# Attention and routed experts on one core: the planner models TensorE's clock and places filler products in its idle time

## The chip, the cores and the metric

The kernel runs on one core of a Trainium2 chip. The metric is the device time of the whole kernel in microseconds (us). One core has five engines with queues of their own, each worked off in order: TensorE (PE, with its weight loads shown apart as PEld), VectorE (DVE), ScalarE (ACT), GpSimd (POOL) and SyncE (SP), which here only starts transfers. TensorE runs at one of two clock levels, 2.4 or 1.2 GHz; the profile shows the granted share of the full clock as PEclk (1.00 or 0.50).

## The reference

```python
# q, k, v: 8 batches x 8 heads x 576 positions x 64, float32
def attention(q, k, v):
    q_rot, k_rot = rotate(q), rotate(k)          # rotary embedding, tables of cos and sin
    scores = matmul(q_rot, k_rot.T) / sqrt(64)
    attn = exp(scores - max(scores))             # along the keys
    return matmul(attn / (sum(attn) + 1e-9), v)
x = attention(q, k, v)                           # heads side by side: 8 x 576 x 512
for b in range(8):
    s = x[b] @ w_gate
    top = argpartition(-s, 128)[:128]            # 128 of 576 rows
    y = maximum(x[b, top] @ w1, 0) @ w2          # 512 -> 1024 -> 512
    out[b] = x[b]
    out[b, top] += sigmoid(s[top])[:, None] * y
```

## The kernel before

The work is cut into 32 pairs of heads (8 batches with 4 pairs each). For one pair, `load` brings q, k and v to SBUF, `rotate` applies the rotary embedding on POOL (on DVE for the first pair), and `turn_qk` transposes q and k on TensorE and splits them into a high and a low part (ACT, POOL, DVE), so that three fast products give a float32 result. `attend` then works in nine units of 128 query rows: `units` makes the scores of two units at a time (twelve products, line 569), `softmax` takes the maximum of each row on DVE (line 586) and the exponential on ACT (line 590), and DVE transposes the exponentials in 32x32 blocks (`turn`, line 604). What a block transpose can't do is done by six transfers from SBUF to SBUF, the moves (`move`, line 617, tile `pt`): two first, and two others that wait for these. Then come the value products (`value`, line 646, float32): per pair one group `c=0` and one group `c=1`, each of 36 products on quarters of the array, which the trace shows as 72 MATMUL records, for one float32 product makes two. The result is copied (line 302), transposed back (line 690) together with the gate's products (line 691), and scaled by DVE (lines 701 to 713). There is one `pt` tile of each kind, so the DVE transposes of the next pair wait until the value products have read it. After every fourth pair `route`, `chosen` and `experts_of` select the 128 rows of a batch and send them through the two expert layers (line 911).

No engine's order is written by hand. Every step is an `Op` with the time that its engine is taken by it, the time until its result is there, a key (a due time) and the steps that it needs. `Order.run` plays the whole kernel through with these costs and lets each engine, whenever it is free, take the ready step with the lowest key; the instructions are then issued in the order so found. A step marked urgent (the score units and the softmax) that is soon ready may keep an engine waiting: another step is taken only if it ends at most `over` ns after that moment. The plan decides the order only; on the chip, semaphores decide the times. In PSUM there are eight banks. A step that needs one asks for kind "t" (one bank, from banks 2 to 7) or kind "s" (a pair of banks); the planner gives out the bank that has been free longest, and the program makes TensorE wait until that bank's last reader is through.

The planner's costs that matter here: a group of value products takes `9 * (228 + 55 * c)` ns, so 2.05 us for `c=0` and 2.55 us for `c=1`; a move takes SP 620 ns, and is counted as landed 2000 ns after it is issued; 256 instructions of TensorE are fetched as one block, which is counted as 3900 ns.

```python
o = op({"SP": (620, 2000)},
       lambda: nc.sync.dma_start(flat[32 * to:32 * to + 32, w_to], flat[32 * at_:32 * at_ + 32, w_at]),
```

Of the kernel before, what the change touches and what calls it, by code (L numbers as in the profile page):

```python
# [19 lines left out]
EPS = 1e-9  # L20


KEY = dict(ahead=8500, lag=13000, rem=400, value=4300, rows=3000, load=22300, rotate=115700, half=2500,
           gate=11700, route=58400, count=35500, select=12400, turn=17500, step=7600, kstep=2700, hold=3,
           patience=900, over=300, near=-300, swap=6000, vsplit=9, vstep=0, recip=6000, pool_lo=1, esplit=2, s_pairs=(0, 1, 2, 3), t_banks=(2, 3, 4, 5, 6, 7), t_most=4)

# [12 lines left out]
class Order:  # L39
# [3 lines left out]

    SEM = 45.0
    BLOCK, FETCH = 256, 3900.0
    PER_KB = 3.6


# [22 lines left out]
    def run(self):  # L71
        import heapq

        names = ("PE", "ACT", "DVE", "POOL", "SP")
        free = {e: 0.0 for e in names}
        mode, shared = 0, 0.0
        count, fetched, moving = 0, 0.0, 0.0
        waiting = {e: [] for e in names}
        idle = [0.0] * (2 * self.pairs)
        held = {}  # L80

        def frees(kind):
            if kind == "s":
                return sorted(max(idle[2 * i:2 * i + 2]) for i in KEY["s_pairs"])
            if sum(x >= 1e12 for x in held.values()) >= KEY["t_most"]:
                return []
            return sorted(idle[i] for i in KEY["t_banks"])

        def take(kind):
            if kind == "s":  # L90
                i = min(KEY["s_pairs"], key=lambda i: max(idle[2 * i:2 * i + 2]))
                idle[2 * i] = idle[2 * i + 1] = 1e12
            else:
                i = min(KEY["t_banks"], key=lambda i: idle[i])
                idle[i] = held[i] = 1e12
            return i

        def give(b, t):
            if b.kind == "s":
                idle[2 * b.slot] = idle[2 * b.slot + 1] = t  # L100
            else:
                idle[b.slot] = held[b.slot] = t

        events = [0.0]
        order = []

        def arrive(o):
            for e in o.engines:
                heapq.heappush(waiting[e], (o.key, o.seq, o))
            heapq.heappush(events, o.ready)  # L110

        for o in self.ops:
            if not o.waits:
                arrive(o)
        while events:
            t = heapq.heappop(events)
            while events and events[0] <= t:
                heapq.heappop(events)
            moved = True
            while moved:  # L120
                moved = False
                for e in names:
                    if free[e] > t:
                        continue
                    put, found, soon, first = [], None, None, None
                    while waiting[e]:
                        item = heapq.heappop(waiting[e])
                        o = item[2]
                        if o.done:
                            continue  # L130
                        can, new = o.ready, {}
                        for b in o.banks:
                            if b.slot is None:
                                new[b.kind] = n = new.get(b.kind, 0) + 1
                                at_ = frees(b.kind)
                                can = max(can, at_[n - 1] if n <= len(at_) else 1e12)
                            elif b.last != e:
                                can = max(can, b.free)
                        if can > t:
                            if o.urgent and can < t + KEY["patience"] and (soon is None or can < soon):  # L140
                                soon = can
                        elif soon is None or t + o.engines[e][0] <= soon + KEY["over"]:
                            if e != "PE" or o.mode == mode or o.urgent and first is None:
                                found = o
                                break

                            if first is None:
                                until = o.key + KEY["near"]
                            if first is None or self.TURN.get((mode, o.mode), 0.0) < self.TURN.get((mode, first.mode), 0.0):
                                first = o  # L150
                        put.append(item)
                        if first and o.key > until:
                            break
                    for item in put:
                        heapq.heappush(waiting[e], item)
                    found = found or first
                    if found is None:
                        if soon is not None:
                            heapq.heappush(events, soon)
                        continue  # L160
                    o, moved = found, True
                    if o is first:
                        o.done = True
                    takes, lasts = o.engines[e]
                    begin = t
                    if e == "DVE" and o.mode == 2:
                        begin = max(t, free["POOL"])
                        shared = begin + takes
                    elif e == "POOL":
                        begin = max(t, shared)  # L170
                    if e == "PE":
                        begin += self.TURN.get((mode, o.mode), 0.0) + 70.0 * (t > free[e] + 1)
                        mode = o.mode
                        n, end = o.size, begin
                        while n:
                            if count % self.BLOCK == 0:
                                end = max(end, fetched)
                                fetched = end + self.FETCH
                            step = min(n, self.BLOCK - count % self.BLOCK)
                            end += takes * step / o.size  # L180
                            n, count = n - step, count + step
                        begin += max(0.0, end - begin - takes)
                    if e == "SP":
                        moving = max(moving, begin + takes) + self.PER_KB * o.size
                        begin += max(0.0, moving - begin - takes)
                    for b in o.banks:
                        if b.slot is None:
                            b.slot = take(b.kind)
                    o.done, o.start, o.end = True, t, begin + lasts
                    order.append((t, len(order), o, e))  # L190
                    free[e] = t + takes if e == "SP" else begin + takes
                    heapq.heappush(events, free[e])
                    for b in o.banks:
                        b.left -= 1
                        b.end = max(b.end, o.end)
                        b.last, b.free = e, b.end + self.SEM
                        heapq.heappush(events, b.free)
                        if not b.left:
                            give(b, b.end + self.SEM)
                            heapq.heappush(events, b.end + self.SEM)  # L200
                    for n in o.outs:
                        n.ready = max(n.ready, o.end + self.SEM)
                        n.waits -= 1
                        if not n.waits:
                            arrive(n)
        assert all(o.done for o in self.ops)
        return order
# [24 lines left out]
def attention_moe_kernel(ctx: ExitStack, tc: tile.TileContext, q, k, v, gate, w1, w2, rope, outs, shape, cap):  # L232
# [17 lines left out]
    nc = tc.nc  # L250
# [19 lines left out]
    def sb(name, shape, dtype=F32):  # L270
        return const.tile(shape, dtype, name=name)
# [6 lines left out]
    order = Order(4)  # L278
    op = order.op
# [26 lines left out]
    def bank_of(b):  # L306
        return banks[:, b.slot] if b.kind == "t" else banks[:, 2 * b.slot:2 * b.slot + 2]


    ident = sb("ident", [P, P])  # L310
    make_identity(nc, ident)
    tabs = sb("tabs", [P, 3, NS, D // 2])
# [30 lines left out]
    rows = ring("row", 1, [P, S])  # L343
# [202 lines left out]
    def attend(pi):  # L546
# [64 lines left out]
        def move(c, key, turns):  # L611
# [1 line left out]
            flat = pt[c].tile.rearrange("p w m s j -> p w (m s j)")  # L613

            def part(to, w_to, at_, w_at, needs):
                o = op({"SP": (620, 2000)},
                       lambda: nc.sync.dma_start(flat[32 * to:32 * to + 32, w_to], flat[32 * at_:32 * at_ + 32, w_at]),  # L617
                       key, needs, size=144 + 36 * c)
                pt[c].by(o)
                moved[c].append(o)  # L620
                return o
# [102 lines left out]
        step = PAIR / len(UNITS)  # L724
        lag = KEY["lag"]
# [366 lines left out]
```

## Time and profile before

| | |
|---|---|
| median of 3 runs | 699.35 us (699.29 to 708.92) |
| the profiled execution | 699.43 us, of which 697.7 us from the first to the last instruction |
| mean granted TensorE clock | 0.951 |
| instructions | 19908, of which PE and PEld 7696 each |

The span is what the trace covers; 1.7 us lie around it. Busy times are unions of an engine's records; TensorE's ends are modelled, so its busy time holds some waiting. A group of rows names the engine's line, the tiles written and read, the idle time before and what ended it.

### The profile page before, as it was taken

How to read it: one execution, taken by the hardware profiler on the slowest of the kernel's cores; microseconds unless marked ns; L12 is line 12 of the kernel's file. 1: busy time of each engine (PE TensorE's matmuls, PEld its weight loads, DVE VectorE, ACT ScalarE, POOL GpSimd, SP SyncE). 2: the span in 40 equal slices, each digit the busy share in tenths (PEclk: the TensorE clock that was granted, in tenths of full speed). 3: DMA queues.
4: the chain of work that ended last, by engine and by line, in shares of the span. 5: the costliest groups of instructions: out<-in, count | busy, mean ns of one | idle time of the engine just before them, and what ended most of it. 6: DMA issues, size and time to landing. Idle time of an engine off the chain costs nothing.

```text
span 697.7 us, 19908 instructions
## 1 busy us (share of the span) xinstructions
PE 583.9 (84%) x7696; PEld 489.8 (70%) x7696; DVE 543.9 (78%) x1350; ACT 362.1 (52%) x958; POOL 424.5 (61%) x489
## 2 busy tenths in 40 slices
PE   4768678888888896899888898899979997899786
PEld 2657566777777775777777786777767786677665
DVE  6677548798789887897878968898788978889351
ACT  2456456555555555465654546465564656454111
POOL 1898689787687477367495368761986378510101
PEclk9998888999899999999999999999999999999999
DMA  5577686678684766668585757757696676636310
GB/s 186 150 200 199 199 247 168 195 191 211 177 232 134 201 184 180 176 168 237 142 217 161 200 152 210 195 148 192 175 247 164 190 194 177 164 92 169 111 35 30
DMA packets 45950, 122.12 MB, mean 175 GB/s; under 512 B 8864, under 2 KB 18080, under 8 KB 45856
## 3 DMA queue, kind: packets, MB, share of 16 engines
q1 hardware_dynamic: 44432, 116.17, 61.0%
q0 software_dynamic: 1280, 4.20, 2.1%
q8 instruction: 61, 1.00, 0.6%
q10 hardware_dynamic: 144, 0.49, 0.2%
q14 instruction: 33, 0.27, 0.1%
HBM read 45.58 MB, written 11.53 MB: 82 GB/s over the span
## 4 chain that ended last, share of the span: by engine, by line
PE 34%; DVE 23%; DMA 17%; issue 9%; ACT 7%; POOL 6%; SPq 3%; POOLq 0%; DVEq 0%; ACTq 0%
PE ps L646 18%; DMA pt<-pt 14%; DVE pt L604 9%; DVE nm L586 8%; PE ps L569 6%; PE ps L911 5%; ACT pab L590 4%; SPq L617 2%; PE ps L477 2%; DVE junk L792 2%; PE ps L690 1%; POOL m L415 1%; DMA xe<-out_dram,idx 1%; PE ps L691 1%; POOL rq L415 1%
## 5 line engine op out<-in xcount | busy, mean ns | idle before, releaser
L590 ACT ACTIVATE pab<-ps,nm 128x576 f32<-128x576 f32 x256 | 187.5, 739 | 124.2 <-DVE nm L586 123.7
L646 PE MATMUL ps<-pt,vt 64*64 64x128 f32 (+1 forms) x4608 | 205.4, 313 | 42.4 <-DMA pt<-pt 17.2
L646 PEld LDWEIGHTS ps<-pt,vt 64*64 64x64 f32 x4608 | 177.5, 147 | 63.8 <-issue 24.8
L604 DVE STREAM_TRANSPOSE pt<-pab 128x576 f32<-128x576 f32 x256 | 185.5, 752 | 42.9 <-PE ps L646 23.1
L586 DVE TENSOR_REDUCE nm<-ps 128x1 f32<-128x576 f32 x288 | 201.6, 737 | 13.3 <-PE ps L569 12.8
L415 POOL TENSOR_TENSOR rk<-k_in,m 128x512 f32<-128x512 f32 (+1 forms) x62 | 52.8, 869 | 104.8 <-PE ps L477 101.9
L569 PE MATMUL ps<-kh,qh 64*128 64x288 f32 (+1 forms) x576 | 94.7, 350 | 20.9 <-ACT pab L590 17.7
L569 PEld LDWEIGHTS ps<-kh,qh 64*128 64x128 f32 (+1 forms) x576 | 56.3, 193 | 51.6 <-ACT pab L590 25.6
L569 PE MATMUL ps<-kh,ql 64*128 64x288 f32 (+1 forms) x576 | 76.7, 305 | 2.9 <-POOL ql L492 2.9
L569 PE MATMUL ps<-kl,qh 64*128 64x288 f32 (+1 forms) x576 | 76.0, 303 | 0.0
L302 ACT COPY ot<-ps 64x64 f32<-64x64 f32 (+1 forms) x112 | 28.2, 281 | 91.1 <-PE ps L646 90.3
L415 POOL TENSOR_TENSOR rq<-q_in,m 64x64 f32<-64x64 f32 (+1 forms) x93 | 57.8, 636 | 12.5 <-PE ps L477 7.7
L492 POOL TENSOR_TENSOR kl<-xf,kh 128x512 fp32r<-128x512 f32 x31 | 39.7, 1280 | 39.9 <-PE ps L646 12.8
L415 POOL TENSOR_TENSOR m<-k_in,tabs 128x320 f32<-128x320 f32 x62 | 53.0, 868 | 17.6 <-DVE rq L415 15.8
L690 PE MATMUL ps<-ident,ot 128*128 128x128 f32 x160 | 47.2, 307 | 19.6 <-ACT pab L590 19.0
L569 PEld LDWEIGHTS ps<-kh,ql 64*128 64x128 f32 (+1 forms) x576 | 58.6, 195 | 4.1 <-POOL ql L492 4.0
L569 PEld LDWEIGHTS ps<-kl,qh 64*128 64x128 f32 (+1 forms) x576 | 58.9, 196 | 0.0
L911 PE MATMUL ps<-w,xt 128*128 128x512 f32 x192 | 51.0, 405 | 2.3 <-DVE xt L888 1.6
L911 PE MATMUL ps<-w,ht 128*128 128x512 f32 x192 | 51.8, 407 | 0.5 <-DVE ht L937 0.5
L590 ACT ACTIVATION_READ_ACCUMULATOR pab<-ps,nm 128x1 f32 x256 | 50.7, 198 | 0.0
L690 PEld LDWEIGHTS ps<-ident,ot 128*128 128x128 f32 x160 | 30.6, 191 | 28.0 <-ACT pab L590 23.0
L691 PEld LDWEIGHTS ps<-wg,ot 128*128 128x128 f32 x320 | 49.1, 209 | 1.3
(103 smaller groups left out, 865.5 us busy)
## 6 DMA issues: line engine op xcount, KB each, us to landing
pt<-pt SPq DMA_DIRECT2D x192, 180.0 KB, 3.7
pt<-pt SPq DMA_DIRECT2D x192, 144.0 KB, 3.7
vt<-v_dram SPq DMA_DIRECT2D x32, 576.0 KB, 5.3
k_in<-k_dram SPq DMA_DIRECT2D x32, 320.0 KB, 4.2
q_in<-q_dram SPq DMA_DIRECT2D x32, 288.0 KB, 4.1
out_dram<-x SPq DMA_DIRECT2D x16, 512.0 KB, 4.2
xe<-w_dram SPq DMA_DIRECT2D x8, 256.0 KB, 4.3
row<-w_dram SPq DMA_DIRECT2D x8, 256.0 KB, 4.9
```

The costliest lines, as they stand in the source:

```text
L302: nc.scalar.copy(out, in_)
L415: lambda: e.tensor_tensor(out, in0, in1, op=alu), key, after)
L477: nc.tensor.transpose(bank_of(b)[:, i * P:i * P + P], r.tile[:, t].rearrange("p h d -> p (h d)"), ident)
L492: d = op({"POOL": pool(n)}, lambda: nc.gpsimd.tensor_tensor(lo, xf.tile, hi.bitcast(F32), op=ALU.subtract), key, [c, y] + lu.before)
L569: nc.tensor.matmul(bank_of(bs[i])[:, n, 0:HALF], lt, rt, start=first, stop=last)
L586: lambda: nc.vector.tensor_reduce(nm.tile[:, u:u + 1], bank_of(b)[:, :, 0:HALF], axis=AX.XY, op=ALU.max, negate=True),
L590: lambda: nc.scalar.activation(dst.rearrange("p (n c) -> p n c", n=2), bank_of(b)[:, :, 0:HALF], AF.Exp, bias=nm.tile[:, u:u + 1], scale=1 ...
L604: lambda: nc.vector.transpose(pt[c].tile[:, 0:2, :, to, :].rearrange("p w m j -> p m w j"), src.rearrange("p (m w j) -> p m w j", w=2, j=32)),
L646: nc.tensor.matmul(bank_of(acc)[64 * h:64 * h + 64, g, :].rearrange("p (w c) -> p w c", w=2)[:, :, c0:c0 + n], vt.tile[gp_, h, m % 2 * NT ...
L690: nc.tensor.transpose(bank_of(b)[:, i * P:i * P + P], cols, ident)
L691: nc.tensor.matmul(bank_of(b)[:, 400 + 2 * i:402 + 2 * i], cols, wg[:, j, :], start=True, stop=True)
L911: nc.tensor.matmul(bank_of(bank), lhs.tile[:, a, c * P:c * P + P], w[w_][:, c, fs], start=(c == 0 and i == 0), stop=(c == n - 1 and i == 2))
```

## The change

Three things are done, in the planner and in what it hands out.

1. The planner keeps an account of TensorE's clock (`work`): it cuts time into steps of `WINDOW`, adds up how long TensorE was taken in each, and sets a flag `slow` by two shares, `FALL` and `RISE`; while it is set, work on TensorE takes twice as long in the plan.
2. Where TensorE is free and no step is found for it, the planner looks at how long TensorE was taken in the last `WINDOW`. At up to `warm` (0.75) of it, after `warm0` (20 us of the plan) and with a "t" bank free, it makes a new step: one float32 product of 256 columns, of the identity matrix with the rotary tables, into that bank. Nobody reads the result. The plan counts it as 430 ns.
3. A move is counted as landed 2500 ns after its issue, where it was 2000 ns.

No step of the old program is removed, and none but the order of the steps is altered otherwise.

```diff
-KEY = dict(ahead=8500, lag=13000, ...
+KEY = dict(landing=2500, warm=0.75, warm0=20000, warm1=1000000, dummy=430, dcols=256, ahead=8500, lag=13000, ...
+    WINDOW, FALL, RISE = 3413.0, 0.58, 0.88
...
+        share, slow, now = {}, False, 0
+        spent = []
+
+        def work(begin, takes):
+            nonlocal slow, now
+            at_ = begin
+            while takes > 0:
+                w = int(at_ // self.WINDOW)
+                while now < w:
+                    b = share.pop(now, 0.0) / self.WINDOW
+                    slow = b < self.RISE if slow else b < self.FALL
+                    now += 1
+                room = (w + 1) * self.WINDOW - at_
+                step = min(room, takes * (2 if slow else 1))
+                share[w] = share.get(w, 0.0) + step
+                takes -= step / (2 if slow else 1)
+                at_ += step
+            return at_ - begin
...
                     if found is None:
                         if soon is not None:
                             heapq.heappush(events, soon)
-                        continue
+                        if e != "PE" or not KEY["warm"] or not spent or not KEY["warm0"] < t < KEY["warm1"] or left < 1:
+                            continue
+                        recent = sum(max(0.0, b - max(a, t - self.WINDOW)) for a, b in spent[-60:])
+                        if recent > KEY["warm"] * self.WINDOW or not frees("t") or frees("t")[0] > t:
+                            if recent > KEY["warm"] * self.WINDOW:
+                                heapq.heappush(events, t + 100.0)
+                            continue
+                        found = self.op({"PE": (KEY["dummy"], KEY["dummy"] + 165)}, None, 0.0, bank=Bank("t"), size=4)
+                        found.fn = self.idle(found.banks[0])
...
                         begin += max(0.0, end - begin - takes)
+                        longer = work(begin, takes) - takes
+                        takes, lasts = takes + longer, lasts + longer
+                        spent.append((begin, begin + takes))
...
+    def idle(b):
+
+        def dummy():
+            nc.tensor.matmul(bank_of(b)[:, 0:KEY["dcols"]], ident, tabs.rearrange("p a b c -> p (a b c)")[:, 0:KEY["dcols"]], start=True, stop=True)
+
+        return dummy
...
-                o = op({"SP": (620, 2000)},
+                o = op({"SP": (620, KEY["landing"])},
```

## Rows read from the trace of the kernel before

**Rows 1.** The page's first part: busy us (share of the span) and instructions.

```profile
PE 583.9 (84%) x7696; PEld 489.8 (70%) x7696; DVE 543.9 (78%) x1350; ACT 362.1 (52%) x958; POOL 424.5 (61%) x489
```

**Rows 2.** The page's chain that ended last: shares by engine and by line.

```profile
PE 34%; DVE 23%; DMA 17%; issue 9%; ACT 7%; POOL 6%; SPq 3%; POOLq 0%; DVEq 0%; ACTq 0%
PE ps L646 18%; DMA pt<-pt 14%; DVE pt L604 9%; DVE nm L586 8%; PE ps L569 6%; PE ps L911 5%; ACT pab L590 4%; SPq L617 2%; PE ps L477 2%; DVE junk L792 2%; PE ps L690 1%; POOL m L415 1%; DMA xe<-out_dram,idx 1%; PE ps L691 1%; POOL rq L415 1%
```

**Rows 3.** Windows laid on the stretches at half clock: engines' busy us, then PEclk, DMA.

```profile
49.38:56.21 6.83, 4.03 (x55) 3.75 (x59) 3.39 (x9) 3.88 (x9) 6.83 (x8) 0.50 0.73 200
...
400.95:404.37 3.42, 3.42 (x52) 3.23 (x56) 1.13 (x2) 0.00 (x0) 0.00 (x0) 0.50 0.03 9
...
sum 64.85, PE 57.84 PEld 52.12 DVE 23.07 ACT 19.16 POOL 41.59; mean PE 4.13 PEld 3.72 DVE 1.65 ACT 1.37 POOL 2.97
```

**Rows 4.** The same windows, with the value products (line 646) alone.

```profile
49.38:56.21 6.83, 2.29 (x44) 2.29 (x48) 0.50 0.73 200
73.28:80.10 6.82, 4.54 (x72) 4.02 (x72) 0.50 0.93 262
...
182.50:189.33 6.83, 2.77 (x39) 2.62 (x43) 0.50 0.84 231
...
sum 64.85, PE 43.48 PEld 39.27; mean PE 3.11 PEld 2.81
```

**Rows 5.** The chain in order of time, 68 to 82 us.

```profile
65.31 5.49 DMA pt<-pt
70.81 3.52 issue
74.33 4.54 PE ps L646 x72
```

**Rows 6.** The chain in order of time, 390 to 412 us.

```profile
396.47 4.35 DMA pt<-pt
...
400.95 4.80 PE ps L646 x56
405.76 0.98 PE ps L569 x12
...
410.38 1.39 PE ps L911 x6
```

**Rows 7.** TensorE's timeline: a value group `c=0` and one `c=1` at full clock.

```profile
193.06 2.20 PE L646 MATMUL ps<-pt,vt 64*64 64x128 f32 x72
...
502.33 3.25 PE L646 MATMUL ps<-pt,vt 64*64 64x192 f32 x72 [0.41 <-ACT pab L590]
```

**Rows 8.** Timeline of 68 to 82 us, after the value group that starts at 74.33.

```profile
78.94 0.37 ACT L302 COPY ot<-ps 128x256 f32<-128x256 f32 x1 [6.16 <-PE ps L646]
...
80.61 0.42 DVE L701 TENSOR_TENSOR x<-ps,rs 128x256 f32<-128x256 f32 x1 [6.55 <-PE ps L691]
```

**Rows 9.** Windows of 5 us from 20 to 695: TensorE's busy time, PEclk, DMA.

```profile
25.00:30.00 5.00, 2.27 (x34) 1.00 0.77 187
...
690.00:695.00 5.00, 2.40 (x11) 0.95 0.00 0
sum 675.00, PE 574.11; mean PE 4.25
```

**Rows 10.** The moves (line 617): issue to landing.

```profile
DMA to landing us min/median/max: 2.3/3.7/6.9
```

**Rows 11.** TensorE's waits: us in total, times, longest.

```profile
PE ps L690 <- ACT pab L590: 19.0, 17, 1.7
PE ps L569 <- ACT pab L590: 17.7, 19, 4.4
PE ps L646 <- DMA pt<-pt: 17.2, 14, 2.8
```

**Rows 12.** Windows of 20 us: busy PE, PEld, DVE, ACT, POOL, then PEclk, DMA.

```profile
40.00:60.00 20.00, 14.03 (x216) 12.12 (x207) 14.82 (x31) 10.96 (x28) 19.37 (x21) 0.83 0.69 191
...
400.00:420.00 20.00, 19.05 (x239) 16.15 (x241) 13.72 (x37) 9.14 (x24) 12.14 (x13) 0.91 0.60 162
```

More of the change, by code (lines that the diff above doesn't have):

```diff
@@ L20 @@
 EPS = 1e-9
-KEY = dict(ahead=8500, lag=13000, rem=400, value=4300, rows=3000, load=22300, rotate=115700, half=2500,
+KEY = dict(landing=2500, warm=0.75, warm0=20000, warm1=1000000, dummy=430, dcols=256, ahead=8500, lag=13000, rem=400, value=4300, rows=3000, load=22300, rotate=115700, half=2500,
            gate=11700, route=58400, count=35500, select=12400, turn=17500, step=7600, kstep=2700, hold=3,
@@ L105, in run @@
         order = []
+        left = len(self.ops)
         def arrive(o):
@@ L188, in run @@
                             b.slot = take(b.kind)
+                    left -= o.fn.__name__ != "dummy"
                     o.done, o.start, o.end = True, t, begin + lasts
@@ L307, in bank_of @@
         return banks[:, b.slot] if b.kind == "t" else banks[:, 2 * b.slot:2 * b.slot + 2]
+    def idle(b):
+        def dummy():
+            nc.tensor.matmul(bank_of(b)[:, 0:KEY["dcols"]], ident, tabs.rearrange("p a b c -> p (a b c)")[:, 0:KEY["dcols"]], start=True, stop=True)
+        return dummy
+    order.idle = idle
     ident = sb("ident", [P, P])
```

## The prediction, made before the changed kernel ran

> **What bounds the kernel now.** I read the page's shares first. TensorE is busy for 84% of the span and DVE for 78% [rows 1], so neither has much room, but the chain that ended last is a mixture: PE 34%, DVE 23%, DMA 17%, and its two longest single entries are the value products, 18%, and the moves that feed them, 14% [rows 2]. What bounds a pair is thus a loop: exponentials, block transposes, moves, value products, and back to the block transposes through the single `pt` tiles.
>
> Then the clock. The windows were laid on the places where the granted clock is 0.50. Leaving out the last one, after the final product, there are 14 stretches with 64.85 us together, in which TensorE is busy for 57.84 us [rows 3]. 43.48 us of this are value products [rows 4], which is the point to see: the clock falls when TensorE has waited for the moves, and what then runs at half clock is just the group that the loop has been waiting for. The chain shows it twice: a move, a wait, and then 4.54 us of value products at 74.33, or a move and 4.80 us of them at 400.95 [rows 5, 6]. At full clock such a group takes 2.20 us (`c=0`) or 3.25 us (`c=1`) [rows 7]. While the slow group runs, ACT stands for 6.16 us and DVE for 6.55 us up to its results [rows 8]; in the stretch from 400.95 on, DVE is busy for 1.13 of 3.42 us and ACT and POOL for nothing [rows 3]. So time saved there is time on the path, unlike most of TensorE's idle time.
>
> **The change part by part.** The sum is made against the profiled execution, 699.43 us; the median of the runs, 699.35, is the same for this purpose.
>
> *Clock, the gain.* At full clock the 43.48 us of value products in these stretches would take about half, so 21.7 us are to be had at most from the loop. Not all of it stays saved. The six stretches before 190 us hold 19.28 us of it (the first and the last of them are shown) [rows 4], and there POOL is busy for up to 19.37 of 20 us and would end last soon after; later it is busy for 12.14 [rows 12]. I count the early half-saving of 9.6 us at half, 4.8 us, and the later one, (43.48 - 19.28) / 2 = 12.1 us, in full: 16.9 us if every fall goes. The remaining 14.4 us of other TensorE work in the stretches I count at nothing: it runs beside DVE and ACT.
>
> How many falls go? A filler can stand only where the planner sees TensorE idle. It counts a move as landed after 2.0 us, now 2.5 us, while the trace has 2.3 us at the least, 3.7 us at the median and 6.9 us at the most [rows 10]. So the planner sees the wait ahead of a value group, but too short a one, by some 1.2 us for each of two moves in series; the rest stays bare idle time, as does the 3.52 us of "issue" ahead of 74.33 [rows 5], which the trace puts down to nothing that the planner has. I take 65% of the falls as gone, because the planned part of the wait comes directly ahead of the group that matters: -11 us. The ends: two falls in ten gone (-3 us), and all of them gone with nothing lost to POOL (-21.7 us).
>
> *Fillers, the cost.* The trace has no such product. Its nearest rows: 36 products of 128 columns on quarters of the array in 2.20 us, so if four quarters work at a time, 9 x 128 columns in 2.20 us, which is 0.49 us for 256 columns; the `c=1` group gives the same, 9 x 192 in 3.25 us and 0.48 us [rows 7]. A bound from below are the expert products, six of 512 columns in 1.39 us, 0.12 us for 256 columns in their faster type [rows 6]; at half clock the upper bound is 0.98 us. I take 0.49. Their number: of 135 windows of 5 us, 31 have TensorE busy for less than 3.75 us (first and last shown), and they lack 21.95 us of three quarters [rows 9], so 45 fillers. At most all idle time from 20 us on is filled: 675 - 574.1 = 101 us, 206 fillers. I take 70, nearer to the lower count, because the rule stops at three quarters: 34 us of TensorE time. Most of it lies in time in which TensorE would wait anyway. What costs is the last filler of a gap, which a step that is ready meets halfway: some 50 gaps x 0.25 us = 12 us, and of these what is on the path, by PE's share of the chain, 34% [rows 2]: +4 us. If that cover is gone altogether, the whole 34 us stand on TensorE's queue; the lower end is 0, for a filler gives nothing back but the clock. Behind a filler are queued whatever TensorE has next, above all the score units, which the planner used to keep TensorE free for; behind those wait DVE's maxima and ACT's exponentials.
>
> A filler also takes a PSUM bank, and has to wait for that bank's last reader, an ACT or DVE copy. It is the bank that has been free longest, so I count nothing; it is part of the slower rival.
>
> *Moves counted 500 ns later.* No instruction changes; the planner puts value groups later among TensorE's steps and may put a unit or a transpose ahead of them. TensorE waits for moves at the head of a value group 14 times, 17.2 us in all, 2.8 us at the longest [rows 11]. If other ready work stood there for 0.5 us each time, 7 us would be gained. Against it, a unit group put ahead of a value group that is ready after all delays the loop by 0.98 us [rows 6]; ten of 64 groups would cost 10 us. I take a gain of 2 us, because the measured landing is far later than either count. The same goes for SP: its queue order shifts a little between moves, loads and stores, for which I have no price beyond these ends.
>
> *The planner's own clock* adds no instruction. It makes the plan longer in places where the old one was too short; I count it with the order.
>
> Sum: -11 + 4 - 2 = -9 us, so 699.4 - 9 = 690 us.
>
> **The rivals.** *All falls go.* If the planned wait ahead of the value groups is filled enough to hold the clock everywhere, and the order round the moves gains its better half: -21.7 + 4 - 5, so 677 us. For it speaks that nearly every fall has the same place in the loop, against it that the longest waits are those that the planner doesn't foresee.
>
> *The falls stay.* The fillers end before the bare wait begins, and the clock falls as before; the gain is -3 us, the cost +4, and the time 699 to 701 us. The landing rows speak for it.
>
> *Slower: fillers ahead of ready work.* The planner's TensorE is faster than the chip's: it counts a `c=1` group at 2.55 us where the trace has 3.25, and a `c=0` group at 2.05 where it has 2.20 [rows 7]; over 32 pairs that is 27 us by which TensorE lags the plan unless a wait takes it up. Where the plan shows an idle TensorE, the chip's may still be at work, and then a filler delays what follows by its whole 0.49 us. The mechanism decides from 29 such fillers on the path on, for 29 x 0.49 = 14 us is what the clock can give; with 60 of them, and the clock's 11 us and the order's 2 us, the time is 699.4 + 29 - 13 = 715 us. Against it speaks that TensorE waits for ACT's exponentials 36 times in the two largest rows alone, 36.7 us [rows 11], so the lag is mostly taken up.
>
> *The fillers don't hold the clock.* Then only their cost is left, +4 to +8 us, about 705 us. In this trace ordinary float32 products do bring the clock back: in the stretch from 73.28 to 80.10 us the 72 value products are 4.54 us of TensorE's work [rows 4], and it ends at full clock. The Trainium skill, "TensorE: Matmul & The Clock Gate", Part 4: PE-mode transpose, says that transposes by TensorE do not count as its being busy in the same way. A filler multiplies with the identity as a transpose does; by that rule, if it applied to fillers, the result would be the 705 us of this rival. Fillers are issued as ordinary products, and no row here isolates a transpose, so the rule gets a small chance only.
>
> **How the numbers follow.** The forecast, 690 us, has a chance of 0.47, with its own range from 682 to 698. All falls gone, 677 us: 0.22. The falls stay, 700 us: 0.16. Fillers ahead of ready work, 715 us: 0.09. No hold, 705 us: 0.06. Two per cent, about what a measurement of this kernel can tell from no change, are 685.4 and 713.3 us. Below the first lie nearly all of the 677 us case and a quarter of the forecast's: 0.34. Above the second lie most of the 715 us case and a little of the others: 0.10. Within: 0.56. The range is to leave out two in ten: from 670 us (the 677 us case with the order's full 7 us) to 709 us, past the case without hold and short of the slower one.
>
> **What the profile after would show.** The mean clock rises from 0.951 to about 0.98, and windows at 0.50 hold some 25 us instead of 64.85. The value products' share of the chain falls from 18% to some 15%, and no group of them takes over 4 us where a filler stands ahead of it. New products `ps<-ident,tabs` appear, 70 of them (140 records), about 0.49 us apart where several follow each other. TensorE's waits for moves shrink by a few us only. The prediction is wrong on the gain if falls remain right behind fillers, on the count if there are over 150 fillers, on the cost if score units wait behind fillers with their inputs long ready, and on the order if the chain's share of moves or of DVE grows by more than the value products give back.

## The result: 2 to 3.5% faster, and the profile after

The changed kernel takes 678.04 us at the median (676.31 to 678.52) against 699.32 us for the kernel before; the ratio is 0.966, with a 95% interval from 0.958 to 0.975. It was measured again beside the last experiments: 683.81 us, ratio 0.981 (0.974 to 0.988). The two intervals barely overlap, so the gain is best read as 2 to 3.5%, some 19 us by the mean of the two ratios. The forecast was 690 us, in a range from 670 to 709 us. Some executions of a kernel take over 1.5% longer than its fastest one: medians are of all executions, ratios and mean clocks over several runs are of the others.

First the page of the kernel after (span 674.6 us, the fastest of its runs): TensorE's busy time and the chain, to be held against [rows 1, 2]. By the new line numbers, 687 are the value products, 610 the score products, 645 the block transposes, 627 the row maxima, 952 the expert products, 345 the fillers.

```profile
PE 585.3 (87%) x7828; PEld 492.9 (73%) x7828; DVE 543.9 (81%) x1348; ACT 361.9 (54%) x960; POOL 424.4 (63%) x489
...
PE 39%; DVE 19%; DMA 16%; issue 8%; POOL 7%; ACT 7%; SPq 3%; POOLq 0%; DVEq 0%; ACTq 0%
PE ps L687 16%; DMA pt<-pt 10%; DVE pt L645 8%; PE ps L610 7%; DVE nm L627 6%; PE ps L952 6%; ACT pab L631 4%; PE ps L518 3%; SPq L658 3%; DMA xe<-w_dram 3%; PE ps L731 2%; DMA xe<-out_dram,idx 2%; PE ps L345 2%; POOL w L1018 1%; POOL m L456 1%
```

TensorE is busy for 585.3 us, 1.4 us more than before, although 28 us of fillers (counted below) are in it: the other work takes 27 us less. About 17 us of that can be had from the 34 us fewer at half clock (below), for half of them is saved at full clock; this is an estimate. Some 7 us are not the clock: without the fillers and with as many falls as before, experiment 1 has 577.2 us where the kernel before has 583.9. The moves' share of the chain fell from 14% of 698 us to 10% of 675 us, 30 us, and that of the value products from 18% to 16%, some 18 us.

The fillers, from the view of line 345 and from TensorE's timeline (start us, us, what):

```profile
L345 PE MATMUL ps<-tabs,ident x132: 377/379/635, 22.3 to 669.3; 128*128 128x256 f32 x132
...
107.90 2.33 PE L345 MATMUL ps<-tabs,ident 128*128 128x256 f32 x10
```

132 records are 66 fillers. Five in a row (ten records, 0.38 us each, overlapping) take 2.33 us, so one record follows another after (2.33 - 0.38) / 9 = 0.22 us, and a filler takes 0.43 us.

The windows on all stretches at half clock, of all work and then of the value products alone; the one after the last product is left out, as in [rows 3, 4].

```profile
133.03:139.86 6.83, 5.90 (x86) 5.57 (x88) 0.06 (x4) 0.37 (x1) 6.67 (x7) 0.50 0.71 179
...
sum 30.71, PE 29.78 PEld 26.89 DVE 11.09 ACT 13.29 POOL 21.92; mean PE 3.72 PEld 3.36 DVE 1.39 ACT 1.66 POOL 2.74
...
sum 30.71, PE 19.25 PEld 18.55; mean PE 2.41 PEld 2.32
```

Eight falls are left of 14, and 30.71 us at half clock of 64.85. Of value products 19.25 us lie there, where it was 43.48. This is the fastest run of the program, though. The profile of its second measurement (experiment 9) has 13 falls, by the same two views:

```profile
sum 51.17, PE 48.13 PEld 42.30 DVE 28.55 ACT 23.73 POOL 28.84; mean PE 3.70 PEld 3.25 DVE 2.20 ACT 1.83 POOL 2.22
...
sum 51.17, PE 27.17 PEld 24.82; mean PE 2.09 PEld 1.91
```

So the number of falls is not the same in each run: of the 14 in the kernel before, six are gone in one profile and one in the other. TensorE's waits in the first profile, for [rows 11]:

```profile
PE ps L687 <- DMA pt<-pt: 8.8, 9, 3.9
...
PE ps L610 <- ACT pab L631: 5.0, 6, 1.4
```

The wait of the value products for the moves is halved (17.2 to 8.8 us), and that of the score products for ACT is down from 17.7 to 5.0 us. So far two stories fit: the clock, or a better order of the steps.

### The profile page after: what moved, and what is told of

Read it like the earlier page. It is cut to its first block, busy times and chain, and to the rows that moved or that the text cites. A ratio compares the mean times of both kernels' runs of the same rounds, so it can differ in the third digit from the quotient of the medians.

```text
span 674.6 us, 20156 instructions
## 1 busy us (share of the span) xinstructions
PE 585.3 (87%) x7828; PEld 492.9 (73%) x7828; DVE 543.9 (81%) x1348; ACT 361.9 (54%) x960; POOL 424.4 (63%) x489
## 4 chain that ended last, share of the span: by engine, by line
PE 39%; DVE 19%; DMA 16%; issue 8%; POOL 7%; ACT 7%; SPq 3%; POOLq 0%; DVEq 0%; ACTq 0%
PE ps L687 16%; DMA pt<-pt 10%; DVE pt L645 8%; PE ps L610 7%; DVE nm L627 6%; PE ps L952 6%; ACT pab L631 4%; PE ps L518 3%; SPq L658 3%; DMA xe<-w_dram 3%; PE ps L731 2%; DMA xe<-out_dram,idx 2%; PE ps L345 2%; POOL w L1018 1%; POOL m L456 1%
## 5 line engine op out<-in xcount | busy, mean ns | idle before, releaser
L687 PE MATMUL ps<-pt,vt 64*64 64x128 f32 (+1 forms) x4608 | 189.6, 300 | 25.2 <-DMA pt<-pt 8.8
L687 PEld LDWEIGHTS ps<-pt,vt 64*64 64x64 f32 x4608 | 164.7, 139 | 46.1 <-ACT pab L631 14.8
L610 PE MATMUL ps<-kh,qh 64*128 64x288 f32 (+1 forms) x576 | 88.0, 343 | 6.1 <-ACT pab L631 5.0
L610 PEld LDWEIGHTS ps<-kh,qh 64*128 64x128 f32 (+1 forms) x576 | 52.9, 192 | 34.7 <-issue 17.8
L610 PE MATMUL ps<-kh,ql 64*128 64x288 f32 (+1 forms) x576 | 72.0, 298 | 0.9 <-POOL ql L533 0.9
L610 PE MATMUL ps<-kl,qh 64*128 64x288 f32 (+1 forms) x576 | 71.9, 297 | 0.0
L610 PEld LDWEIGHTS ps<-kh,ql 64*128 64x128 f32 (+1 forms) x576 | 54.7, 191 | 1.1 <-POOL ql L533 1.1
L610 PEld LDWEIGHTS ps<-kl,qh 64*128 64x128 f32 (+1 forms) x576 | 55.0, 191 | 0.0
```

Source lines behind the costliest of these rows:

```text
L610: nc.tensor.matmul(bank_of(bs[i])[:, n, 0:HALF], lt, rt, start=first, stop=last)
L687: nc.tensor.matmul(bank_of(acc)[64 * h:64 * h + 64, g, :].rearrange("p (w c) -> p w c", w=2)[:, :, c0:c0 + n], vt.tile[gp_, h, m % 2 * NT ...
```

## The experiments

Each kernel was timed beside the kernel before on the same chip. Beside each stands the mean granted clock of its profiled run; the kernel before has 0.951 in its own.

**1. The order of the changed kernel, its fillers not issued.** The plan is made with the fillers, so each engine's steps stand as in the changed kernel.

```diff
         def dummy():
-            nc.tensor.matmul(bank_of(b)[:, 0:KEY["dcols"]], ident, ...
+            pass
```

> The changed kernel's order step for step, planned with the fillers, but the 66 fillers themselves are not issued. Clock theory (the gain is value products that no longer run at half clock): the falls come back, mean clock near 0.95, and some 14 to 20 us of the 21 us are lost, 692 to 698 us. Order theory (the gain comes from the other order of the steps, the fillers are at best free): 675 to 681 us, because 35 us of fillers on TensorE are gone as well.

Measured: 684.83 us, ratio 0.979 (0.974 to 0.985), clock 0.948. Neither theory alone: 14 falls are there again, and a gain of 2.1%, 14 us, all the same. This is the order, on a clock no better than that of the kernel before. The sums of the windows on its 14 half-clock stretches, all work and the value products alone, are close to those of the kernel before:

```profile
sum 68.27, PE 62.34 PEld 55.48 DVE 34.21 ACT 25.21 POOL 49.85; mean PE 4.45 PEld 3.96 DVE 2.44 ACT 1.80 POOL 3.56
...
sum 68.27, PE 44.42 PEld 40.42; mean PE 3.17 PEld 2.89
```

Its waits show what the order alone does:

```profile
PE ps L610 <- ACT pab L631: 9.7, 12, 2.5
...
PE ps L687 <- DMA pt<-pt: 6.8, 9, 1.6
```

The value products' wait for moves fell from 17.2 to 6.8 us without a filler, so this part of the change in the waits is the order's. The score products' wait for ACT fell from 17.7 to 9.7 us by the order; the 5.0 us of the kernel after have the fillers too.

**2. Moves counted 500 ns later, alone.** No fillers, no account of the clock.

```diff
-            ... landing=2500, warm=0.75, ...
+            ... landing=2500, warm=0, ...
-                        longer = work(begin, takes) - takes
+                        longer = 0.0
```

> Moves counted as landed after 2500 ns, no fillers, no account of the clock in the plan. Clock theory: 694 to 700 us, mean clock near 0.95, since nothing holds the clock. Order theory: most of the gain is here, 680 to 688 us, and the chain's share of the moves falls from 14% to about 10%.

Measured: 708.13 us, ratio 1.009 (1.003 to 1.014), clock 0.940. The later landing by itself gains nothing; the chain's share of the moves stays at 14%. The order theory as put there falls.

**3. Fillers alone.** Moves at 2000 ns, no account.

```diff
-            ... landing=2500, ...
+            ... landing=2000, ...
-                        longer = work(begin, takes) - takes
+                        longer = 0.0
```

> Fillers by the same rule, moves counted at 2000 ns as before, no account of the clock in the plan. Clock theory: 678 to 686 us, mean clock about 0.97. Order theory: 693 to 700 us.

Measured: 692.52 us, ratio 0.983 (0.978 to 0.988), clock 0.971. The fillers alone give 1.7%, 12 us, a little less than the 13 to 21 us that the clock theory had expected. The plan makes 82 of them here (164 records), in an order of its own, whose price is in this time too (experiment 12).

**4. Fillers and account, moves at 2000 ns.** The first half of the diff of experiment 3 alone.

> The changed kernel with the moves counted as landed after 2000 ns again; fillers and account stay. If the later landing is worth the 2 us of the prediction: 678 to 682 us. If it carries the change (order theory): 690 us or more.

Measured: 705.74 us, ratio 1.013 (1.006 to 1.019), at a clock of 0.967. The clock is held, and yet the kernel is slower than before: an order can cost more than the clock gives. The 2 us that the prediction had put on the landing are far off when it is combined with the other two parts.

**5 and 6. The changed kernel with moves at 2400 and at 2600 ns.**

```diff
-            ... landing=2500, ...
+            ... landing=2400, ...
```

> The changed kernel with the moves counted as landed after 2400 ns. If the gain of the order is a truer count of the moves, 100 ns less move the time by less than 0.5%: 675 to 683 us against 699 for the kernel before. If the order's part is scatter (the list planner falls into another of many orders with any small change of a cost), the ratio lies anywhere between 0.97 and 1.01.

> The same with 2600 ns. Truer count: 674 to 682 us, at least as fast as 2500 ns, since the measured median is 3.7 us. Scatter: anywhere between ratios of 0.97 and 1.01, without a trend from 2400 over 2500 to 2600.

Measured: 679.79 us, ratio 0.976 (0.967 to 0.985), clock 0.980, and 683.02 us, ratio 0.978 (0.970 to 0.985), clock 0.975. From 2400 to 2600 ns the gain stays within the intervals of the two measurements at 2500 ns. So it is no single lucky order, but none of the three is faster than another beyond its interval either, and "at least as fast as 2500 ns" is not shown for 2600.

**7. Fillers and later moves, no account of the clock.** The second half of the diff of experiment 2 alone.

> Fillers and moves at 2500 ns, but the plan's products take as long as before (no account of the clock). If the account matters, the time is that of fillers and landing alone, 685 to 700 us; if it is idle, within 0.5% of the changed kernel, 675 to 682 us. In either case the mean clock should be 0.97 or more, because the fillers are there.

Measured: 691.43 us, ratio 0.992 (0.988 to 0.996), clock 0.983, the best clock of these and still over 1% behind the changed kernel. On the same chip the kernels with the account and moves at 2400 and 2600 ns have 0.976 and 0.978, clear of its interval. The account matters, through the order.

**8. Account and later moves, no fillers in the plan.** The first half of the diff of experiment 2 alone.

> Account and moves at 2500 ns, but the plan has no fillers at all. The plan then sees its own TensorE slow down and nothing holds the chip's clock: mean clock near 0.95. If the order gains by these two alone, about 685 us, as the order with fillers left out; if the order was luck of the plan with fillers, 695 to 708 us.

Measured: 706.11 us, ratio 1.010 (1.006 to 1.015). Without fillers in the plan, its order is not the one of experiment 1, and the gain is gone. The mean clock of its runs is 0.929, lower than in the kernel before.

**9. The changed kernel again**, without an edit, as the yardstick of the next three.

> The changed kernel once more, as the yardstick of the three others on the same chip: a ratio of 0.96 to 0.975 to the kernel before, some 679 us, mean clock 0.976.

Measured: 683.81 us, ratio 0.981 (0.974 to 0.988), clock 0.962: outside of what was expected, by little. One program's clock is not the same in each run: here from 0.962 to 0.970, in the first measurement from 0.967 to 0.976.

**10. Every filler issued twice**, with the same plan.

```diff
         def dummy():
-            nc.tensor.matmul(bank_of(b)[:, 0:KEY["dcols"]], ident, ...
+            for _ in range(2):
+                nc.tensor.matmul(bank_of(b)[:, 0:KEY["dcols"]], ident, ...
```

> Same plan and order, but every filler is issued as two products, 132 instead of 66, which adds 66 x 0.43 = 28 us of TensorE's work. If the fillers lie in waits that TensorE has anyway: at most 4 us more than the changed kernel, and a clock of 0.98 or more. If they stand in front of ready work, as the slower rival has it: by the share of TensorE in the chain (39%) 11 us more, up to 28 us more, 690 to 706 us.

Measured: 690.83 us, ratio 0.991 (0.986 to 0.995), clock 0.977; that is 7 us above experiment 9 at a better clock, between what the two expectations had. The intervals of the two just overlap. Of the 28 us more of TensorE's work, about a quarter shows in the time, but the better clock hides some: by the line of the next section the mean clock of 0.977 beside 0.965 is worth 5 us, so up to 12 us of the 28 may be on the path. Most of this work still lies in waits. The page's chain has them with 5% now, 2% in the changed kernel (its line is 346 here).

```profile
PE ps L688 19%; PE ps L611 9%; DVE pt L646 7%; DMA pt<-pt 7%; DVE nm L628 6%; PE ps L953 6%; PE ps L346 5%; ACT pab L632 5%; PE ps L519 4%; PE ps L732 2%; DMA xe<-out_dram,idx 2%; SPq L659 2%; DVE junk L834 1%; PE ps L733 1%; DMA xe<-w_dram 1%
```

**11. Fillers as transposes**, four of 128 columns each, same plan.

```diff
-            nc.tensor.matmul(bank_of(b)[:, 0:KEY["dcols"]], ident, ...
+            for i in (0, 1, 0, 1):
+                nc.tensor.transpose(bank_of(b)[:, i * P:i * P + P], tabs...[:, i * P:i * P + P], ident)
```

> Same plan and order, but each filler is four transposes of 128 columns (about 0.11 us each, so about the same time as the float32 product of 256 columns). If transposes count as work for the clock as products do: mean clock 0.97 to 0.98 and the time of the changed kernel. If they do not: mean clock near 0.95 and the time of the order without fillers, some 7 us more.

Measured: 684.40 us, ratio 0.983 (0.976 to 0.991), beside 0.981 in experiment 9. By time this is no gain over the order without fillers either (0.979 in experiment 1). The clock is what tells the two expectations apart: in the profiled runs 0.970 (span 680.6 us) with transposes, 0.962 (682.0 us) with products in experiment 9, and 0.948 (682.5 us) in the order without fillers; over four runs each, 0.960 to 0.970, 0.962 to 0.970, and 0.948 to 0.956. In the fillers' places, among TensorE's other work, transposes hold the clock as the products do.

**12. The order of experiment 3, its fillers not issued.** The diffs of experiments 3 and 1 together.

> The order of the run with fillers alone (moves at 2000 ns, no account), but the fillers are not issued. It repeats the test of a fixed order on another order: if the issued fillers are worth 1 to 1.5% through the clock, the ratio to the kernel before is 0.995 to 1.0 where that run had 0.983, and the mean clock falls from 0.971 to about 0.945. If the order alone had the gain, the ratio stays at 0.98.

Measured: 703.35 us, ratio 1.007 (1.003 to 1.011), clock 0.935. With fillers the same order had 0.983 (0.978 to 0.988). The intervals lie far apart: in this order the issued fillers are worth 2.4%, 16 us net of their own cost, while the clock goes from 0.935 to 0.971.

## Why the prediction was right, and where it was not

The direction and the range were right, and so was the mechanism that issued fillers raise the clock and that a higher clock saves time. The term of the clock was too large. The term of the order was mis-sized, and it is the larger one. That the time lies in the range is partly luck: clock and cost together came to some -5 us where -7 stood in the sum, and most of the gain is an order for which 2 us had been put down. The same kind of edit gave 1.009 to 1.013 of the time of the kernel before in experiments 2, 4 and 8.

**The clock.** The step was -11 us, for 65% of the falls gone. Six of 14 went in the first profiled execution, with 34 of 65 us at half clock, and one of 14, with 14 us, in the second. The picture behind the step was too narrow: not "nearly every fall has the same place in the loop". By TensorE's timeline the longest wait next to the fall (counted from 5 us ahead of its start to 2 us behind it) is one of the value products for moves, or an unassigned one ahead of them, at seven of the 14 falls in the kernel before; in the order of experiment 1 it is so at one of 14. Of the eight falls that are left in the first profile, two are next to waits for moves; at the six others the wait ended with a result of ACT or POOL. One of the two, at 133.03 us, begins inside TensorE's longest wait for moves, 3.9 us, which follows four filler records and two of value products; and the fall at 27.22 us begins while fillers run. So the prediction's sign of being wrong on the gain, falls right behind fillers, came up in part.

The price can be had from rows of one and the same kernel: its clock differs a little from run to run, and the time with it. The runs of the kernel before on three chips, 50 in all, go from 695.43 us at 0.966 to 705.53 us at 0.947 on the first chip, from 691.70 us at 0.966 to 701.16 us at 0.947 on the second; a straight line through all, each chip's about its own mean, has 3.9 us for 0.01 of mean clock, with a 95% interval of 2.8 to 5.0. It is a correlation: a run whose waits are longer for another reason would have a longer time and a lower clock too. The eight runs of the changed kernel have a mean clock of 0.969 and the four of experiment 1 have 0.950, so by the line the fillers' clock is worth 1.9 x 3.9 = 7 us here. In experiment 12 against 3, the mean clock goes from 0.934 to 0.975, and the same line gives 16 us; measured were 16 us, with the fillers' own cost in them. So the mechanism is shown by taking the fillers out of one order, and the size there agrees with the line; in the changed kernel's own order 7 us are an estimate from the line and not shown, because the direct comparison, 0.979 without fillers and 0.966, 0.981 and (as transposes) 0.983 with them, does not settle it.

**The fillers' cost.** 70 of 0.49 us were assumed; there are 66 of 0.43 us, 28 us of TensorE instead of 34. The net cost, +4 us, is not measured by itself. In experiment 10, a second set of fillers costs 7 us, or up to 12 with the clock's part taken out; what order and clock leave over (next paragraph) is 2 us for the first set. The step is of the right size as far as this goes.

**The order.** This is the step that failed: "I take a gain of 2 us". Experiment 1 has 14 us in the order alone, and experiment 4 shows an order that loses 1.3% with the clock held. Order -14 and clock -7 make -21 us, beside -19 by the mean of both measurements of the changed kernel; the 2 us between them are the remainder named above, and no check of the sum. The mistake was to price three edits of the planner's costs each by its own small displacement. They act together: with all three the ratio is 0.966 to 0.981, with any two, or with the fillers or the landing alone, 0.983 to 1.013 (the account alone was not run). The fillers alone, 0.983, are not clear of the 0.981 of the second measurement. An order's price also has its clock in it: the kernels of experiments 2, 8 and 12 run at mean clocks of 0.944, 0.929 and 0.934 where the kernel before beside them has 0.955, 0.955 and 0.953, and by the line this makes 4, 10 and 7 us of the 6, 7 and 5 that they lose. Experiment 4 loses its 9 us at a better clock than the kernel before.

Where this order gains is seen when each trace is divided at the same pieces of work, from the last row maximum of the 9th pair to that of the 14th; a first window holds this stretch, a second goes on to the last pair's. Kernel before, experiment 1, and both profiles of the kernel after:

```profile
187.70:294.50 106.80, 92.31 (x1283) 77.19 (x1275) 87.89 (x220) 56.36 (x154) 69.74 (x82) 0.98 0.66 183
294.50:645.00 350.50, 313.83 (x4310) 264.43 (x4311) 298.10 (x729) 195.79 (x522) 206.91 (x235) 0.97 0.67 180
```

```profile
186.10:282.10 96.00, 84.18 (x1234) 71.35 (x1230) 85.35 (x212) 55.48 (x152) 64.31 (x76) 0.98 0.71 202
282.10:630.80 348.70, 314.09 (x4329) 264.10 (x4333) 299.72 (x734) 196.19 (x526) 209.92 (x238) 0.98 0.68 181
```

```profile
183.50:278.40 94.90, 85.21 (x1239) 72.16 (x1232) 85.23 (x211) 55.30 (x152) 64.30 (x76) 0.98 0.72 202
278.40:624.00 345.60, 313.77 (x4357) 264.44 (x4361) 300.19 (x734) 196.39 (x526) 209.99 (x238) 0.99 0.69 183
```

```profile
183.10:280.20 97.10, 87.37 (x1246) 73.73 (x1238) 85.57 (x212) 55.78 (x152) 64.67 (x76) 0.96 0.69 200
280.20:631.20 351.00, 318.71 (x4357) 268.21 (x4361) 300.23 (x735) 196.39 (x526) 209.53 (x238) 0.97 0.68 179
```

These five pairs take 106.8 us in the kernel before and 96.0 us in the order of the changed kernel without fillers, at the same clock of 0.98: 10.8 of the 14 us. The next 18 pairs are nearly even (350.5 and 348.7 us). The first profile of the kernel after is 7.9 us shorter than that of experiment 1, 3.1 us of it in these 18 pairs, at 0.99, and 2.6 us ahead of the first window; in its second profile, at 0.96 and 0.97, both windows are a little longer than in experiment 1.

Two rows differ in the first stretch. The expert products, line 911 before and 952 in experiment 1, are fewer, 60 and 42: 6 of the 18 stand ahead of the stretch in experiment 1 and 12 behind it. And the engines' idle time before instructions that write or read `pt`, put down to a move, falls from 7.0 us to 1.0. Neither row is the cause by itself, as the traces of two other experiments show. Experiment 7 has 60 expert products there, and its stretch takes 96.8 us (its row is the third here):

```profile
187.70:294.50 106.80, 16.33 (x60) 10.57 (x60) 0.98 0.66 183
```

```profile
186.10:282.10 96.00, 11.42 (x42) 7.39 (x42) 0.98 0.71 202
```

```profile
187.80:284.60 96.80, 16.21 (x60) 10.62 (x60) 0.96 0.68 187
```

Experiment 12 has the same 7.0 us of idle time for moves as the kernel before (one line in both traces; the second is experiment 1), and its stretch takes 91.5 us, though its whole time is longer than that of the kernel before:

```profile
  DMA pt<-pt: 7.0, 7
```

```profile
  DMA pt<-pt: 1.0, 2
```

And the order of experiment 6 gains elsewhere: 103.5 us in this stretch, but 173.6 us ahead of it, where the kernel before has 187.7. So why this order is faster stays open, and so does why only the three parts together lead to such orders. Moves at 2400 to 2600 ns do, at 2000 ns they don't, so the step's thought that a truer landing gives a better order may be right, but only in a plan that also has the fillers and the slow clock in it (experiments 2, 7 and 8). That several small changes of a cost fall into good or bad orders by chance is a rival that these runs don't rule out; the expectation of experiment 5 put its range at 0.97 to 1.01, and both 0.976 and 0.978 lie in it.

**The rivals.** The time of "all falls go", 677 us, came out in the first measurement, but not its mechanism: eight falls are left there, 13 in the second. "The falls stay" is ruled out by the windows. "Fillers ahead of ready work" is real at the size of the cost term; its 715 us would have needed 60 of them on the path, 29 us, where doubling all 66 cost 7 to 12 us. (Its 14 us for "what the clock can give" don't fit the prediction's own 16.9 us for all falls.) "The fillers don't hold the clock" is ruled out twice, by experiments 1 and 12 through the clock, and for transposes by experiment 11. The rule of the Trainium skill that stood behind this rival ("TensorE: Matmul & The Clock Gate", Part 4: PE-mode transpose) does not hold here even for fillers that are transposes, with a clock of 0.970 where it is 0.948 without them; no run here has a long stretch of transposes alone.

**What the profile was to show.** Mean clock about 0.98: 0.976 in the first profile, 0.962 in the second. Some 25 us at half clock: 30.7 and 51.2. The value products' share some 15%: 16% and 15%. 140 records of fillers: 132. Waits for moves smaller by a few us: by 8.4 and 5.7 us, and by 10.4 us in experiment 1 without a filler. The sign that was given for an order gone wrong, a larger share of moves or DVE in the chain, came out the other way in the first profile (14% to 10% for the moves, 23% to 19% for DVE); in the second they have 11% and 25%.

## What to carry to other kernels

Filler products can pay where TensorE's idle time lies directly ahead of work that everything else waits for (2.4% in the order of experiment 3; in the changed kernel's own order no gain is shown directly): look at what runs in the half-clock stretches, and whether it is on the chain, before counting all of them, and take more than one profile, for the number of falls in one program went from 8 to 13 here. When a change goes through a planner, issue the same order without the added work; this run splits a gain into order and mechanism, which no comparison of the two traces did. And take a planner's order as a term of its own of a per cent or two in either direction: edits of a cost that looked like 2 us moved this kernel between 0.966 and 1.013 of its time.

## What the runs showed of the hardware that was not expected

Transposes on TensorE, issued in waits among other work, hold the granted clock like ordinary products (mean clock 0.970, beside 0.962 with products and 0.948 with nothing in the same places). And the mean granted clock of one unchanged program on one core varies from run to run, from 0.944 to 0.966 for the kernel before, with 3.9 us of its time for each 0.01: a good part of the scatter between runs of this kernel goes with its clock, and the changed program had 8 falls in one profile and 13 in another.
